# Windowed attention and a gated FFN on one core: two token tiles on one weight chunk, 24 float32 heads, decode moved beside the FFN

## The chip, the cores and the metric

One core of a Trainium2 chip. The metric is the device time of one launch in microseconds (us), the median of several runs. A profiled execution has a span, from its first to its last instruction, and its own device time, a little longer than that span.

## The reference, cut to what matters

Attention over 8 batches and 8 heads of size 64: 512 local tokens that see the 32 global tokens and a window of 32 on each side, and 32 global tokens that see everything. The 4608 x 512 result goes through an FFN whose weights have 512 x 2048 and 2048 x 512 numbers.

```python
s_ll = np.where(np.abs(pos[:, None] - pos[None, :]) <= 32, scale * q_l @ k_l.T, -1e9)
a_l = sm(np.concatenate([scale * q_l @ k_g.T, s_ll], axis=-1))
out_l = a_l @ np.concatenate([v_g, v_l], axis=2)
out_g = sm(scale * q_g @ k_all.T) @ v_all
x = np.concatenate([out_g, out_l], axis=2)        # then to 4608 x 512
h = x @ w_in
r = np.maximum(h, 0.0)
g = s * (r * r) + b
return g @ w_out
```

## The kernel before

**Units of work.** A slot j is one head on one half (256 rows) of a batch's local tokens: 128 slots, 16 to a batch. A tile t is 256 token rows of x, so eight slots fill one tile; tile 16 holds all the global tokens. The FFN runs in 136 steps m, eight to a tile: `ffn_in(m)` makes 256 hidden units of the tile (24 matmuls into PSUM tile `ps_h`), ACT takes the relu (`r`), DVE squares and scales it, ACT and DVE split it into a high and a low part (`g`), and `ffn_out(m)` adds it into two output accumulators (12 matmuls into `acc`). `ffn_out(m - 1)` stands behind `ffn_in(m)`, and slot j = m + 10 (`LAG`) is worked on beside step m.

**Two kinds of heads.** Slots from 16 (`NF`) on are split: each operand becomes a high and a low float32r part by an ACT copy and a DVE or POOL subtraction (`split`, `v_split`, `p_split`), and PE multiplies the parts. The first 16 slots, batch 0, go as float32, two heads at a time (`scores32`, `transposes32`, `pv32`): no splits, and ACT scales the probabilities.

**Weights.** They arrive as 64-bit words and are decoded on the chip (`weight_piece`): 32 pieces of 512 columns, each a 512 KB load, an ACT pass over the middle bits (L147), three DVE passes (L148, L151, L152), an ACT copy to the high part (L156) and a DVE subtraction for the low part (L157). All of `wi` and `wo` is used in the first eight steps, since those run through all hidden units of tile 0.

**Order.** Tile waits follow from the buffers. Up to slot 19 a scheduler orders every engine's queue at build time; from slot 20 (`ORDERED`), step 10, PE takes the order of the code. Every engine works its queue in order. [...] SP issues the loads, and each load waits for the eighth one before it to land. `keep_busy` runs matmuls on constants at the start.

## Time and profile before

| | |
|---|---|
| median of 3 runs | 1034.72 us (1034.71 to 1036.84) |
| the profiled execution's own time | 1035.21 us, 1.81 us more than its span |
| its span | 1033.4 us |
| PE busy | 998.6 us (97%) |
| DVE, ACT, POOL busy | 813.8 (79%), 710.4 (69%), 300.2 us (29%) |
| mean granted TensorE clock | 0.979 of full speed |

A line of the page's fifth part gives a group of equal instructions: line, engine, tile written <- tiles read, shape, count, then busy time, mean duration, and idle time before it with who ended that. A digit in a row of slices is the busy share in tenths. Durations of ACT and DVE overlap a little when they run back to back, so the distance from start to start is what one costs there.

### The profile page before, as it was taken

To read this page: it belongs to the slowest core of one execution; us is meant where nothing else is said; L and a number is where in the kernel's file an instruction comes from. 1 tells how busy PE (TensorE), PEld (TensorE's weight loads), DVE (VectorE), ACT (ScalarE), POOL (GpSimd) and SP (SyncE) were. 2 spreads that over 40 slices of the span, in tenths; PEclk is the share of its full clock that TensorE was granted. 3 is DMA by queue.
4 is the path that set the end of the run, shared out by engine and by line. 5 is a ranking of instruction groups with operands and counts; after the bars stand their busy time and mean duration, and the time that the engine had idled before them with its cause. 6 is when DMAs were issued, how large, how long until landed. Compare 5 with 4: busy or idle time off the path is not lost.

```text
span 1033.4 us, 20334 instructions
## 1 busy us (share of the span) xinstructions
PE 998.6 (97%) x7060; PEld 904.7 (88%) x7060; DVE 813.8 (79%) x2096; ACT 710.4 (69%) x1816; POOL 300.2 (29%) x365
## 2 busy tenths in 40 slices
PE   7779989999999999999999999999999999999996
...
GB/s 301 248 219 151 89 91 73 72 59 90 88 73 54 72 87 76 79 61 90 74 79 56 77 83 67 79 67 87 75 75 58 95 72 44 43 24 35 12 21 21
DMA packets 62254, 85.73 MB, mean 83 GB/s; under 512 B 7368, under 2 KB 49352, under 8 KB 62152
## 3 DMA queue, kind: packets, MB, share of 16 engines
...
q10 hardware_dynamic: 288, 1.05, 0.3%
...
## 4 chain that ended last, share of the span: by engine, by line
PE 85%; ACT 5%; DVE 5%; DMA 3%; issue 1%; SPq 0%; DVEq 0%; ACTq 0%
PE ps_h L499 34%; PE acc L532 34%; PE ps_t L308 5%; PE ps_o L380 4%; PE ps_s L355 4%; PE ps_og L451 2%; DMA wst<-in_w_out 2%; PE ps_g L359 1%; ACT sm L219 1%; ACT wst L147 1%; DVE g L514 1%; DVE x L393 1%; DMA b_t<-in_bv 1%; DVE r L506 1%; ACT g L513 1%
## 5 line engine op out<-in xcount | busy, mean ns | idle before, releaser
L499 PE MATMUL ps_h<-xs,wi 128*128 128x256 f32 x3264 | 419.3, 284 | 0.0
L532 PE MATMUL acc<-wo,g 128*128 128x512 f32 x1632 | 405.0, 395 | 0.5 <-ACT g L513 0.5
L499 PEld LDWEIGHTS ps_h<-xs,wi 128*128 128x128 f32 x3264 | 397.1, 190 | 3.3 <-issue 0.5
L532 PEld LDWEIGHTS acc<-wo,g 128*128 128x128 f32 x1632 | 294.9, 188 | 56.8 <-ACT g L513 0.8
L514 DVE SCALAR_TENSOR_TENSOR g<-r,b_t,g 128x512 fp32r<-128x512 f32 x136 | 120.3, 885 | 57.6 <-ACT g L513 57.0
L505 ACT ACTIVATE r<-ps_h 128x512 f32<-128x512 f32 x136 | 81.3, 598 | 115.5 <-PE ps_h L499 109.7
L513 ACT ACTIVATE g<-r,b_t 128x512 fp32r<-128x512 f32 x136 | 98.4, 723 | 78.6 <-DVE r L506 78.1
L192 POOL TENSOR_TENSOR kq<-rq,kq 128x256 fp32r<-128x256 f32 x112 | 83.9, 750 | 231.1 <-ACT kq L191 226.7
L506 DVE SCALAR_TENSOR_TENSOR r<-ps_h,s_t,r 128x512 f32<-128x512 f32 x136 | 101.2, 744 | 58.3 <-ACT r L505 58.3
L190 POOL TENSOR_TENSOR kq<-rk,kq 64x416 fp32r<-64x416 f32 x56 | 61.0, 1089 | 264.3 <-ACT kq L189 254.4
L219 ACT ACTIVATE sm<-sm,nm 128x224 f32<-128x224 f32 (+1 forms) x256 | 119.7, 469 | 1.4 <-DVE nm L213 1.0
L200 POOL TENSOR_TENSOR vs<-rv,vs 128x256 fp32r<-128x256 f32 x112 | 91.2, 815 | 51.2 <-ACT vs L199 45.9
L308 PE MATMUL ps_t<-ident,sm 128*128 128x128 f32 (+1 forms) x512 | 96.8, 277 | 7.9 <-DVE pg L433 3.0
L363 ACT COPY tg<-ps_g 32x256 f32<-32x256 f32 (+1 forms) x112 | 42.3, 378 | 72.3 <-PE ps_g L359 71.7
L380 PE MATMUL ps_o<-pt,vs 128*128 128x256 f32 x448 | 91.0, 285 | 0.0
L213 DVE CUSTOM_DVE_ANT_0 sm<-ps_s,mask 128x192 f32<-128x192 f32 (+1 forms) x224 | 74.6, 370 | 11.2 <-PE ps_s L355 11.0
L443 POOL TENSOR_TENSOR vsg<-rvg,vsg 128x320 fp32r<-128x320 f32 x64 | 57.8, 924 | 77.5 <-ACT vsg L442 77.5
L391 DVE TENSOR_TENSOR u<-ps_o,u 128x256 f32<-128x256 f32 x112 | 47.3, 422 | 41.8 <-ACT u L390 40.0
L355 PE MATMUL ps_s<-kq 128*128 128x192 f32 (+1 forms) x448 | 78.4, 266 | 0.0
L355 PEld LDWEIGHTS ps_s<-kq 128*128 128x128 f32 x448 | 72.0, 190 | 6.8
L308 PEld LDWEIGHTS ps_t<-ident,sm 128*128 128x128 f32 (+1 forms) x512 | 58.4, 145 | 13.3 <-ACT ptp L315 4.6
L228 DVE TENSOR_SCALAR sm<-sm,ss 128x192 f32<-128x192 f32 (+1 forms) x224 | 68.0, 346 | 1.0
...
## 6 DMA issues: line engine op xcount, KB each, us to landing
rq<-in_qd SPq DMA_DIRECT2D x112, 128.0 KB, 2.3
rv<-in_vw SPq DMA_DIRECT2D x112, 128.0 KB, 2.1
...
wst<-in_w_in SPq DMA_DIRECT2D x15, 512.0 KB, 4.3
wst<-in_w_out SPq DMA_DIRECT2D x15, 512.0 KB, 4.3
...
```

The source lines that it names most:

```text
L192: nc.gpsimd.tensor_sub(out=qs[:, 1, :], in0=rq, in1=f32(qs[:, 0, :]))
L200: nc.gpsimd.tensor_sub(out=vs[:, :, 1, :], in0=rv4, in1=f32(vs[:, :, 0, :]))
L219: nc.scalar.activation(out=p, in_=p, func=AF.Exp, bias=nm[:, n:n + 1], scale=-1.0, accum_out=ss[:, n:n + 1],)
L308: nc.tensor.transpose(out=p_t[:, at:at + q], in_=sm[0:q, c0:c0 + P], identity=ident[0:q, 0:q])
L355: nc.tensor.matmul(p_s[:, cols], lhsT=qs[:, a, blk * P:(blk + 1) * P], rhs=ks[:, cols], start=(a == 0), stop=(a == 1),)
L380: nc.tensor.matmul(p_o[:, blk, :, q0:q0 + n], lhsT=vs[:, 2 * blk + c], rhs=pt[:, :, o], start=(c == 1), stop=(c == 0),)
L499: nc.tensor.matmul(p_h[:, k], lhsT=wi[:, a, c, f * P:(f + 1) * P], rhs=xs[:, e, c, :], start=(n == 0), stop=(n == 11),)
L505: nc.scalar.activation(out=r, in_=p_h, func=AF.Relu)
L506: nc.vector.scalar_tensor_tensor(out=r, in0=p_h, scalar=s_t, in1=r, op0=ALU.mult, op1=ALU.mult)
L513: nc.scalar.activation(out=g[:, 0], in_=r, func=AF.Identity, bias=b_t)
L514: nc.vector.scalar_tensor_tensor(out=g[:, 1], in0=r, scalar=b_t, in1=f32(g[:, 0]), op0=ALU.add, op1=ALU.subtract,)
L532: nc.tensor.matmul(oacc[t][i], lhsT=g[:, a, k, i * P:(i + 1) * P], rhs=wo[:, e, f, :], start=(pr == 0 and n == 0), stop=(pr == 7 and n == 5),)
```

## The change

- **Two tiles to a chunk.** Steps 0 to 15 (`FIRST`) each take one chunk of 128 hidden units and run it for tiles 0 and 1: the same 24 and 12 matmuls as before, but into four output accumulators. These take the banks `acc0`, `acc1`, `h1` and `o`, so `ps_h` has one bank, `h0`, until step 16. Step m needs chunk m alone.
- **Chunks of 1024 columns.** 16 chunks in place of 32 pieces, 1 MB to a load, each with the same six passes at twice the width (L140 and L151 on ACT, L141, L144, L145, L152 on DVE). Four staging buffers; the load of chunk c + 4 waits for chunk c's last pass. Three chunks (`EARLY`) are called for among the first eight pairs and one at the end of each step from then on.
- **24 float32 slots.** Twelve pairs: eight ahead of step 0, the other four at steps 2, 5, 8 and 11 (scores), one step later (transposes) and one more (product with V). A pair's k, q and v come in one load of 606 KB (`load32`, `pairs`).
- **Order.** PE takes the code's order from step 0 on. Batch 0's global-token work is placed by `G_FIRST`, and V and the temporary of the decode (`wb`) share one buffer. The warming matmuls are 8 at the start and 16 behind the second pair's scores, and the activation table is asked for at the start (`act_first`).
- **Buffers.** `kq`, `rk` and `rq` go from three to two, `xs` from one to two; tiles get other paddings.

```diff
-NF = 16
-AHEAD = 0
+NF = 24
+FIRST = 16
 LAG = 10
-ORDERED = 20
-WARM_FIRST = 28
+WARM_FIRST = 8
+WARM_SECOND = 16
+SPARE = 12
+NCH = 16
+EARLY = (1, 4, 7)
+S32, T32, PV32 = ({3 * i + 2 + k: 8 + i for i in range(4)} for k in range(3))
+G_FIRST = {1: ("load", 0), 3: ("pv", 0), 4: ("pv", 2), 5: ("load", 4), 7: ("pv", 4), 9: ("pv", 6)}
...
+    def weight_load(c):
+        n = c if c >= SPARE else SPARE + c % 4
+        st = weight_tile(n, I32, f"wst{c}")[:, 0:2050]
+        nc.sync.dma_start(st.bitcast(I16)[:, 1:4097], wts[c])
+        st_["w", c] = st
...
+        below = sb.tile([P, 20 * D], I16, tag="rvg", name=f"wb{c}", bufs=1)[:, 0:1024]
...
     def ffn_in(m):
-        t, pr = m // 8, m % 8
-        xs = xs_[t]
-        p_h = ps.tile([P, 2, HALF], F32, tag="h", name=f"ps_h{m}", bufs=2)
+        if m < FIRST:
+            tag, terms = "h0", [(t, m) for t in range(2)]
+        else:
+            tag, terms = f"h{m % 2}", [(m // 8, 2 * (m % 8) + k) for k in range(2)]
+        p_h = ps.tile([P, 2, HALF], F32, tag=tag, name=f"ps_h{m}")
...
+            outs = [(0, i, [(i // 2, m)]) for i in range(4)]
+            tags = ("acc0", "acc1", "h1", "o")
...
+            for t, i, _ in sorted(outs, key=lambda x: -x[1] if m < FIRST else x[1]):
+                o = sb.tile([P, DM + 16], F32, tag="r", name=f"o{t}_{i}", bufs=2)[:, 0:DM]
+                (nc.vector.tensor_copy if i == 2 else nc.scalar.copy)(out=o, in_=oacc[t, i])
...
+    for i in range(10):
+        if i < 8:
+            scores32(i)
+        if 0 <= i - 1 < 8:
+            transposes32(i - 1)
+        if 0 <= i - 2:
+            pv32(i - 2)
+            if i - 2 == 3:
+                x_split(0)
+            elif i - 2 == 7:
+                x_split(1)
+        if i >= 8:
+            g_softmax(0, i - 8)
+        if i in EARLY:
+            next_chunk()
+    fixed.enter_context(tc.manual_schedule(engines={mybir.EngineType.PE}))
...
+        if m < NM:
+            ffn_in(m)
...
         if 0 <= m - 1 < NM:
-            ffn_out(m - 1, turns.pop(j, iter(())))
+            ffn_out(m - 1, turn)
+        list(turn)
+        if m < FIRST:
+            next_chunk()
```

ACT's queue around the first relu of the FFN. `wst` is a staged piece or chunk, `ptp` a pair's transposed probabilities, `xs` the split x, `r0` and `g0` step 0. Before, pieces 0 to 22 stand ahead of `r0`:

```order
L329 COPY x1_669<-ps_op4_660 128x256 [waits DVE_49,PE_49]
L147 ACTIVATE wst22_624<-wst22_624,mid_b_129 128x512 [waits DMAHW2_49]
L156 CAST wo_127<-we19_576 128x512 [waits DVE_49]
L505 ACTIVATE r0_698<-ps_h0_673 128x512 [waits PE_49]
L156 CAST wi_126<-we20_607 128x4x128 [waits DVE_49]
L156 CAST wo_127<-we17_519 128x512 [waits DVE_49]
L315 COPY ptp5_731<-ps_t10_732 128x416 [waits PE_49]
L147 ACTIVATE wst21_615<-wst21_615,mid_b_129 128x512 [waits DMAHW4_49,Activation_49]
L505 ACTIVATE r1_769<-ps_h1_744 128x512 [waits PE_49]
L513 ACTIVATE g0_701<-r0_698,b_t_72 128x512 [waits DVE_49]
```

Now, with chunk 8 of 16 before and chunk 9 behind `r0`, and the last pairs' copies between:

```order
L309 COPY ptp6_536<-ps_t13_543 128x416 [waits PE_49]
L140 ACTIVATE wst8_742<-wst8_742,mid_b_112 128x1024 [waits DMAHW7_49]
L309 COPY ptp7_569<-ps_t14_570 128x416 [waits PE_49]
L151 CAST w5_820<-wst5_401 128x1024 [waits PE_49]
L309 COPY ptp7_569<-ps_t15_576 128x416 [waits PE_49]
L469 CAST xs1_610<-x1_507 128x512 [waits DVE_49]
L506 ACTIVATE r0_650<-ps_h0_625 128x512 [waits PE_49]
L509 ACTIVATE g0_653<-r0_650,b_t_72 128x512 [waits DVE_49]
L140 ACTIVATE wst9_823<-wst9_823,mid_b_112 128x1024 [waits DMAHW1_49,Activation_49]
L506 ACTIVATE r1_693<-ps_h1_668 128x512 [waits PE_49]
```

The first pass over chunks 6, 7 and 8 and the whole of chunks 0 to 5 stand ahead of `r0`; the pass over chunk 9 moved between `g0` and `r1`.

DVE's queue between `r4` and `r5`; `wb`, `we` and `wst` belong to the decode. Before:

```order
L506 SCALAR_TENSOR_TENSOR r4_1057<-ps_h4_1032,s_t_71,r4_1057 128x512 [waits Activation_49]
L157 TENSOR_TENSOR wo_127<-we27_799,wo_127 128x512 [waits Activation_49]
L157 TENSOR_TENSOR wo_127<-we25_723,wo_127 128x512 [waits Activation_49]
L151 SCALAR_TENSOR_TENSOR wst30_915<-wst30_915,we30_916 128x512 [waits DVE_49]
L157 TENSOR_TENSOR wi_126<-we28_808,wi_126 128x4x128 [waits Activation_49]
L190 TENSOR_TENSOR kq16_1075<-rk16_989,kq16_1075 64x416 [waits Activation_49]
L148 TENSOR_SCALAR we31_925<-wst31_924 128x512 [waits DMAHW2_49,DVE_49]
L148 TENSOR_SCALAR we29_907<-wst29_906 128x512 [waits DMAHW1_49,DVE_49]
L152 SCALAR_TENSOR_TENSOR we30_916<-wst30_915 128x512 [waits DVE_49]
L151 SCALAR_TENSOR_TENSOR wst31_924<-wst31_924,we31_925 128x512 [waits DVE_49]
L514 SCALAR_TENSOR_TENSOR g4_1060<-r4_1057,b_t_72,g4_1060 128x512 [waits Activation_49]
L151 SCALAR_TENSOR_TENSOR wst29_906<-wst29_906,we29_907 128x512 [waits DVE_49]
L506 SCALAR_TENSOR_TENSOR r5_1123<-ps_h5_1098,s_t_71,r5_1123 128x512 [waits Activation_49]
```

Now, the last seven rows ahead of `r5` and the four behind it:

```order
L141 TENSOR_SCALAR wb8_1075<-wst8_742 128x1024 [waits DMAHW7_49,DMAHW4_49,Pool_49]
L152 TENSOR_TENSOR w7_993<-wst7_666,w7_993 128x1024 [waits Activation_49]
L144 SCALAR_TENSOR_TENSOR wst8_742<-wst8_742,wb8_1075 128x1024 [waits DVE_49]
L217 TENSOR_SCALAR ss18_1007<-ss18_1007 128x4 [waits Activation_49]
L145 SCALAR_TENSOR_TENSOR wst8_742<-wst8_742 128x1024 [waits DVE_49]
L141 TENSOR_SCALAR wb9_1153<-wst9_823 128x1024 [waits DMAHW1_49]
L218 RECIPROCAL ss18_1007<-ss18_1007 128x4 [waits DVE_49]
L507 SCALAR_TENSOR_TENSOR r5_1050<-ps_h5_1025,s_t_71,r5_1050 128x512 [waits Activation_49]
L144 SCALAR_TENSOR_TENSOR wst9_823<-wst9_823,wb9_1153 128x1024 [waits DVE_49]
L152 TENSOR_TENSOR w8_1080<-wst8_742,w8_1080 128x1024 [waits Activation_49]
L145 SCALAR_TENSOR_TENSOR wst9_823<-wst9_823 128x1024 [waits DVE_49]
L510 SCALAR_TENSOR_TENSOR g5_1053<-r5_1050,b_t_72,g5_1053 128x512 [waits Activation_49]
```

The passes over chunks 6 to 15 and the work of four pairs now stand between the `r` and `g` rows of steps 1 to 13; before, pieces 20 to 31 stood between those of steps 0 to 6.

PE's queue at steps 4 to 6. Before, `ps_h4` and `ps_h5` lie in two banks and follow each other:

```order
L499 MATMUL ps_h4_1032<-xs0_597,wi_126 128x256 [waits DVE_49]
L499 MATMUL ps_h4_1032<-xs0_597,wi_126 128x256 x23
L499 MATMUL ps_h5_1098<-xs0_597,wi_126 128x256 [waits DVE_49]
L499 MATMUL ps_h5_1098<-xs0_597,wi_126 128x256 x5
L323 MATMUL ps_op6_1022<-ptp6_933,rvp6_671 64x128 [waits Activation_49]
L323 MATMUL ps_op6_1022<-ptp6_933,rvp6_671 64x96 x2
L323 MATMUL ps_op6_1022<-ptp6_933,rvp6_671 64x128 x2
L323 MATMUL ps_op6_1022<-ptp6_933,rvp6_671 64x64 x2
L532 MATMUL acc0_0_775<-wo_127,g3_974 128x512 [waits Activation_49]
L532 MATMUL acc0_0_775<-wo_127,g3_974 128x512
L532 MATMUL acc0_1_776<-wo_127,g3_974 128x512 x2
L499 MATMUL ps_h5_1098<-xs0_597,wi_126 128x256 x17
```

Now step 5's and step 6's input halves lie in one bank, and `ps_h6` waits for DVE's `r5`:

```order
L499 MATMUL ps_h5_1025<-xs0_453,w5_820 128x256 x12
L499 MATMUL ps_h5_1025<-xs1_610,w5_820 128x256 x12
L537 MATMUL acc0_0_706<-w4_739,g4_943 128x512 [waits Activation_49]
L537 MATMUL acc0_0_706<-w4_739,g4_943 128x512
L537 MATMUL acc0_0_706<-w4_739,g4_943 128x512 [waits DVE_49]
L537 MATMUL acc0_1_707<-w4_739,g4_943 128x512 x3
L537 MATMUL acc0_2_708<-w4_739,g4_943 128x512 x3
L537 MATMUL acc0_3_709<-w4_739,g4_943 128x512 x3
L499 MATMUL ps_h6_1085<-xs0_453,w6_910 128x256 [waits DVE_49]
L499 MATMUL ps_h6_1085<-xs0_453,w6_910 128x256 x11
L499 MATMUL ps_h6_1085<-xs1_610,w6_910 128x256 x12
```

The input half of a step moved behind the output half of the step two before it, and its first matmul waits for the read of the step before.

## Rows read from the trace of the kernel before

**Rows 1.** The page's slices of the whole span: PE's busy tenths, 40 slices of 25.8 us.

```profile
PE   7779989999999999999999999999999999999996
```

**Rows 2.** Busy time of each engine in stretches of the start: stretch, its length, then PE, PEld, DVE, ACT and POOL busy us (instructions), granted clock, DMA share, GB/s.

```profile
10.00:20.00 10.00, 5.38 (x30) 2.89 (x30) 7.79 (x29) 7.75 (x22) 0.00 (x0) 0.82 1.00 365
...
130.00:140.00 10.00, 6.88 (x41) 5.80 (x40) 7.95 (x17) 7.54 (x19) 5.54 (x7) 0.79 0.41 125
140.00:150.00 10.00, 10.00 (x72) 9.51 (x71) 7.54 (x17) 6.10 (x18) 4.44 (x6) 0.86 0.28 82
```

**Rows 3.** The same view in two longer stretches, same columns.

```profile
20.00:50.00 30.00, 22.50 (x117) 13.99 (x116) 29.51 (x82) 29.79 (x79) 0.00 (x0) 0.67 0.81 267
50.00:70.00 20.00, 15.36 (x108) 12.16 (x107) 19.52 (x49) 18.56 (x43) 0.00 (x0) 0.82 0.69 216
```

**Rows 4.** PE's matmuls in order of time, 133 to 142 us: start us, us, line, out<-in, tile, count, and in brackets the idle time before and who ended it.

```profile
133.46 0.33 PE L359 MATMUL ps_g<-kq,qgs 128*64 128x256 f32 x1
136.24 0.48 PE L428 MATMUL ps_tg<-ident,sg 128*128 128x128 f32 x1 [2.44 <-DVE sg L364]
```

**Rows 5.** PE's matmuls in order of time, 139 to 187 us, same columns; an FFN input half is x24, an output half x12.

```profile
139.68 4.43 PE L499 MATMUL ps_h<-xs,wi 128*128 128x256 f32 x24
...
148.62 3.04 PE L499 MATMUL ps_h<-xs,wi 128*128 128x256 f32 x24
...
182.63 0.47 PE L355 MATMUL ps_s<-kq 128*128 128x224 f32 x3
...
183.17 0.40 PE L380 MATMUL ps_o<-pt,vs 128*128 128x256 f32 x2
...
183.91 3.05 PE L499 MATMUL ps_h<-xs,wi 128*128 128x256 f32 x24
186.79 2.94 PE L532 MATMUL acc<-wo,g 128*128 128x512 f32 x12
```

**Rows 6.** All engines in order of time, the first 14 us: start us, us, engine, line, out<-in, idle before.

```profile
5.69 0.43 DVE L148 TENSOR_SCALAR we<-wst 128x512 int16<-128x512 int16 x1 [4.29 <-DMA wst<-in_w_in]
...
8.89 0.69 DVE L151 SCALAR_TENSOR_TENSOR wst<-wst,we 128x512 int32<-128x512 int16 x1
...
9.51 0.68 DVE L157 TENSOR_TENSOR wi<-we,wi 128x512 fp32r<-128x512 f32 x1
...
10.11 0.68 DVE L152 SCALAR_TENSOR_TENSOR we<-wst 128x512 int32<-128x512 int32 x1
...
10.69 0.43 PE L277 MATMUL ps_sp<-rkp,rqp 64*128 64x192 f32 x1
...
11.32 0.35 PE L277 MATMUL ps_hp<-rkp,rqp 64*128 64x224 f32 x1
...
12.89 0.43 DVE L148 TENSOR_SCALAR we<-wst 128x512 int16<-128x512 int16 x1 [0.73 <-DMA wst<-in_w_in]
13.24 0.35 DVE L213 CUSTOM_DVE_ANT_0 sm<-ps_sp,mask 128x192 f32<-128x192 f32 x1
...
13.63 0.46 ACT L219 ACTIVATE sm<-sm,nm 128x192 f32<-128x192 f32 x1
```

**Rows 7.** ACT in order of time, 36 to 42 us, where it never waits: start us, us, line, out<-in.

```profile
36.08 1.53 ACT L226 ACTIVATE sm<-sm,ss 128x192 f32<-128x192 f32 x4
37.51 0.75 ACT L147 ACTIVATE wst<-wst,mid_b 128x512 int32<-128x512 uint32 x1
38.16 0.60 ACT L156 CAST wi<-we 128x512 fp32r<-128x512 f32 x1
38.67 0.49 ACT L315 COPY ptp<-ps_t 128x416 f32<-128x416 f32 x1
39.07 0.75 ACT L416 ACTIVATE sg<-sg,gm 128x544 f32<-128x544 f32 x1
...
40.93 0.37 ACT L286 COPY sg<-ps_gp 64x288 f32<-64x288 f32 x1
41.21 0.48 ACT L219 ACTIVATE sm<-sm,nm 128x224 f32<-128x224 f32 x1
...
41.69 0.60 ACT L156 CAST wo<-we 128x512 fp32r<-128x512 f32 x1
```

**Rows 8.** The page's DMA issues: line, engine, count, KB each, median us from issue to landing.

```profile
wst<-in_w_in SPq DMA_DIRECT2D x15, 512.0 KB, 4.3
```

**Rows 9.** The chain of work that ended last, in order of time: start us, us, engine, tile, line, count.

```profile
72.86 0.93 PE ps_op L323 x11
...
87.01 0.39 PE ps_t L308 x4
...
117.94 0.60 PE ps_og L451 x10
...
155.82 2.80 PE ps_h L499 x24
...
159.22 2.79 PE acc L532 x12
```

**Rows 10.** The page's costliest groups, two of DVE: line, out<-in, count, busy us, mean ns of one, idle before.

```profile
L514 DVE SCALAR_TENSOR_TENSOR g<-r,b_t,g 128x512 fp32r<-128x512 f32 x136 | 120.3, 885 | 57.6 <-ACT g L513 57.0
...
L506 DVE SCALAR_TENSOR_TENSOR r<-ps_h,s_t,r 128x512 f32<-128x512 f32 x136 | 101.2, 744 | 58.3 <-ACT r L505 58.3
```

**Rows 11.** DVE's groups by shape, 20 to 60 us: line, out<-in, count, busy us, mean ns of one.

```profile
L331 DVE COPY x<-ps_op 128x256 f32<-128x256 f32 x4 | 1.7, 416 | 0.0
```

More of the change, by code (lines that the diff above doesn't have):

```diff
@@ L282, in scores32 @@
         nc.tensor.matmul(
-            p_g[0:64, 0:ng], lhsT=st_["rqg", 0][:, 64 * hp:64 * hp + 64], rhs=own(rk, hf), start=True, stop=True,
+            p_g[0:64, 0:ng], lhsT=st_["rqgp", b][:, 64 * hp:64 * hp + 64], rhs=own(rk, hf), start=True, stop=True,
         )
+        if i == 1:
+            with tc.issue_after(part.ins):
+                keep_busy(WARM_SECOND, "warm1")
         softmax(heads, p_s)
@@ L562, in window_attention_then_ffn @@
                 extra[s0 + G_TR + G_PV[i]].append(lambda b=b, h=h: g_pv(b, h))
-    def pick(pair, split_one):
-        def run(j):
-            if NF <= j < NS:
-                split_one(j)
-            elif 0 <= j < NF and j % 2 == 0:
-                with tc.high_priority(offset=AHEAD):
-                    pair(j // 2)
-        return run
-    ld = pick(load32, load)
-    sp = pick(lambda i: None, split)
-    vl, vl32 = pick(lambda i: None, v_load), pick(v_load32, lambda j: None)
-    sc = pick(scores32, scores)
@@ L577, in window_attention_then_ffn, with pick @@
-    tr = pick(transposes32, lambda j: None)
-    vsp = pick(lambda i: None, v_split)
-    pvs = pick(pv32, lambda j: None)
-    piece = 0
-    qg_load(0)
-    ld(0)
-    ld(2)
-    fixed = ExitStack()
-    for j in range(NM + LAG + 2):
-        if j == ORDERED:
-            fixed.enter_context(tc.manual_schedule(engines={mybir.EngineType.PE}))
+    def pick(run):
+        return lambda j: run(j) if NF <= j < NS else None
+    ld, sp, vl, sc, vsp = (pick(run) for run in (load, split, v_load, scores, v_split))
```

302 lines of the change are left out of this document (161 added, 141 removed).

## The prediction

> **What bounds the kernel now.** I read the slices of the span first [rows 1]: PE's busy share is 9 tenths or more in nearly every slice behind the first six, so there PE is the limit, and a change of the start can only move the moment from which PE runs without a gap. Then the start by stretches [rows 2, 3]: from 20 to 50 us ACT is busy for 29.79 of 30 us and DVE for 29.51, PE for 22.5 at a granted clock of 0.67. ACT and DVE, which decode the weights and do the softmax, set the time there. The last disturbance is near 136 us: PE stands still for 2.44 us behind DVE [rows 4], the mean clock of that stretch is 0.79 and of the next 0.86 [rows 2], and step 10's input half takes 4.43 us where step 11's takes 3.04 [rows 5].
>
> From then on the two programs do the same work on PE, so I compare them at one point: the start of step 15's output half, 186.79 us in the trace of before [rows 5] (the change puts step 16's input half ahead of a product and four transposes there, and I count those in). What the change gains there it keeps to the end.
>
> **Term 1: the first FFN step can start.** Step 0 now needs tiles 0 and 1, so all eight pairs. In the trace of before the first scores run at 10.69 us and end at 11.67, yet DVE reads them at 13.24, behind a decoding pass that waited for its load until 12.89, and ACT's first exponential is at 13.63 [rows 6]. Now the first pair's 606 KB is the first load. The 512 KB piece that was the first load of before was ready at 5.69 [rows 6]; I take 6.0 for the pair, 0.97 for scores and 0.35 for the first DVE pass, and put the first exponential at 7.3.
>
> From there ACT is the longest list ahead of `r0`. The order gives the counts, the distances from start to start the prices [rows 7]: 32 exponentials at 0.48 with their sums (15.4 us), 32 scalings at 0.36 (11.4), 8 score copies at 0.28 (2.2), 16 copies of transposes at 0.40 (6.4), two long exponentials (1.5), four casts of x at 0.51 (2.0), four small V casts (1.3). A decoding pass costs 0.65 and a cast 0.51 for 512 columns. A 288-column copy lasts 0.37 and a 512-column cast 0.60, which is 1.0 ns for each further column, so 1024 columns should cost 1.15 and 1.0; the bounds are one price of 512 and twice that price. Nine passes and six casts: 10.4 and 6.0. Sum 56.6 us. ACT idled 1.65 us in the 50 us from 20 to 70 [rows 3]: 2 more. Behind the last scaling come transposes, two copies, the product, a DVE copy, the last cast and six matmuls, about 3 us beyond what is counted. The input half of step 0 ends at 7.3 + 56.6 + 2 + 3 = **69 us**.
>
> That is hardly earlier than before, where PE's unbroken work begins at 72.86 [rows 8]: "decoded beside the FFN" holds for ten chunks, while six stand whole ahead of `r0` and three more with their first pass. Two things can make it later. A chunk's load is 1 MB: half of it lands in 4.3 us [rows 9], and at the 365 GB/s of 10 to 20 us [rows 2] the other half adds 1.4, so 5.7, bounds 4.3 and 8.6. The pass over chunk 8 stands on ACT ahead of the last pair's copies; its load waits for chunk 4's last pass, some 7 us ahead of it by the list, so it just about hides, and any more is paid. And SP's queue holds nine pairs and four chunks, 9.7 MB, ahead of the small loads and chunk 4: 27 us at that rate, near 36 us with what stands between, when ACT comes to chunk 4. I take 69, from 64 (if part of the nine passes fills gaps that ACT would have had) to 73.
>
> **Term 2: PE's own work from there to the point.** At full clock [rows 8]: 16 input halves at 2.80 (44.8), 15 output halves at 2.79 (41.9). Four pairs: scores 0.97 [rows 6], one more product at 0.35, two times four transposes at 0.39, the product with V at 0.93 [rows 8], 3.03 each, 12.1. Four global products at 0.60 (2.4), ten global transposes at the same 0.39 for four (1.0). Slots 24 to 26: scores at 0.54 and one set of product and transposes at 0.74 [rows 5], with the first four transposes 2.7. Sum **104.9 us**. The eight slots that are no longer split would have cost PE 0.54 and 0.74 each [rows 5], 10.2 in all against the 12.1, so PE's work hardly changes; what falls away is DVE's, ACT's and POOL's splitting.
>
> **Term 3: PE waits for DVE in steps 4 to 13.** Until step 16 `ps_h` has one bank, so a step's input half waits until DVE has read the step before (`r`), and only an output half and a pair's work stand between. DVE prices: at 512 columns 0.62 and 0.60 from start to start, the first pass 0.35 [rows 6]; a 256-column copy lasts 0.42 [rows 11] and a 512-column pass 0.68, again 1.0 ns a column, so the wide passes cost 1.14 and the first 0.62 (bounds 0.6 and 1.24, 0.35 and 0.70). `r` lasts 0.74, `g` 0.89 [rows 10]. From `r4` to `r11` the order has 8 first passes, 25 wide ones, seven `r`, seven `g`, 12 score passes at 0.35 and some 16 small ones: 5.0 + 28.5 + 5.2 + 6.2 + 4.2 + 5 = 54 us. PE's own work from the end of input half 4 to that of 11 is seven steps at 5.59, 8.3 of pairs and 2.3 of global work: 49.7. So 4.3 us of wait at the least. Taken step by step it is more: between `r4` and `r5` DVE has 12.6 us of this against PE's 8.6, and between `r9` and `r11` 20 against 13.6, while in steps 0 to 3 DVE stands idle, because chunk 6 needs the buffer that a load of V fills. With what each piles up I come to 9. I take **6.5**, the middle, bounds 2 and 13.
>
> In the trace of before a queue holds back what is ready behind what is not: the scores of 11.67 waited for a load that they don't need [rows 6]. [...]
>
> **Term 4: the clock.** A stall near 2.4 us was followed by a half at 4.43 in place of 3.04 [rows 4, 5], 1.4 lost. At 69 us PE comes from a stretch like the one before, where the mean was 0.67 to 0.82 [rows 3]. I take **2**, bounds 0 and 6.
>
> [...]
>
> **Term 5: four accumulators are emptied at once.** Two `r` buffers carry four output tiles, so the third waits for the first one's store, and output half 16 for the fourth copy. Between lies a slot's PE work and an input half, 4.1 us. I take **1**, bounds 0 and 3. I put `kq`, `rk` and `rq` with two buffers at nothing: a load that lands in less than the 4.3 us of 512 KB [rows 9] has a step of 6.9 us to do it in, and if that cover were gone each late load would show as a wait of a score.
>
> **The sum.** 69 + 104.9 + 6.5 + 2 + 1 = 183.4, against 186.8: 3.4 us earlier. The profiled execution of 1035.21 would become 1031.8, the median of 1034.72 becomes **1031.3 us**.
>
> **The rivals.** *DVE decides and PE's clock falls* (slower). One bank, and chunk passes ahead of nearly each `r` of steps 4 to 13: 12 us of wait and three falls of the clock, 4.2. Sum 69 + 104.9 + 12 + 4.2 + 1 = 191.1, 1039.0 us. It decides from 11.9 us of waits and clock together on (186.8 less the other terms). For it: DVE's 54 us against 49.7, and the stall at 136 us, also behind DVE. Against it: each step has an output half of 2.79 us [rows 8] between a read and the matmul that waits for it, and over the eight steps DVE's work is only 4.3 us more than PE's.
>
> *The start is short* (faster by much). The passes ahead of `r0` fill gaps of ACT, which waited where I have it busy: 64 for term 1, 4 for term 3, 1 for each other. 174.9, 1022.8 us. For it: the wide passes could cost less than my line from 256 to 512 columns. Against it: ACT's gaps in the trace are 1.65 us in 50.
>
> *The change does not do what it says* (no gain). Chunk 4 or 8 lands late, ACT stands before it with all pairs' work behind, and the start moves to 72.5: 186.9, 1034.8 us. For it: ACT and DVE before waited for such loads until 12.89 [rows 6]. Against it: it needs only 5.7 us of load hidden.
>
> **How the numbers follow.** Forecast 0.36, slower rival 0.28, short start 0.20, no gain 0.16. Measurements of this kernel tell a change of some 0.2% (2.1 us) from none. Of the forecast I count 0.26 as faster, 0.08 as the same and 0.02 as slower, of the last rival 0.12 as the same and 0.04 as slower: faster 0.46, same 0.20, slower 0.34. The likeliest case by itself spans 1027 to 1035. The range for 8 in 10 takes in the short start and the slower rival with half of its bounds: 1022 to 1042.
>
> **What would show it.** The input half of step 0 ends at 64 to 73 us (term 1), ACT above 95% busy from 12 to 65 us. PE's idle time behind `r` (`ps_h` waiting for DVE) in steps 4 to 13 adds up to 2 to 13 us, most of it ahead of steps 6, 11 and 12 (term 3). The clock is below 1 at the start of the FFN and at most twice after it (term 4). Output half 15 starts near 183 us, and the steps behind it last 6.9 us as before; if they are longer, the two-buffer tiles cost what I put at nothing. An input half 0 that ends before 60 us, or waits over 15 us, would prove the sum wrong.

## The result, and the profile after

| | before | after |
|---|---|---|
| median | 1035.78 us (4 runs beside after's) | 1043.38 us (1043.0 to 1044.45, 4 runs) |
| ratio, 95% interval | | 1.0074 (1.0059 to 1.0088) |
| span of the profiled execution | 1033.4 us | 1042.4 us |
| PE, DVE, ACT busy | 998.6, 813.8, 710.4 us | 1007.8, 774.3, 697.7 us |

The change makes the kernel 7.6 us slower; the forecast was 1031.3 us, the range 1022 to 1042. DVE has 39.5 us less to do and ACT 12.7, PE 9.2 more.

Busy time by stretches in the kernel after: stretch, its length, PE, PEld, DVE, ACT, POOL, granted clock, DMA share, GB/s.

```profile
7.30:71.30 64.00, 53.34 (x302) 34.51 (x302) 44.10 (x120) 56.27 (x145) 3.79 (x4) 0.75 0.65 255
20.00:50.00 30.00, 25.48 (x135) 15.84 (x134) 21.15 (x66) 29.31 (x78) 3.79 (x4) 0.67 0.75 291
50.00:70.00 20.00, 15.96 (x106) 12.10 (x106) 12.66 (x27) 14.73 (x35) 0.00 (x0) 0.76 0.26 86
60.00:90.00 30.00, 25.59 (x155) 21.17 (x155) 10.82 (x26) 15.59 (x33) 0.00 (x0) 0.83 0.18 70
...
140.00:160.00 20.00, 17.87 (x123) 14.39 (x121) 19.94 (x31) 13.09 (x26) 2.92 (x2) 1.00 0.34 121
```

Against [rows 3], DVE is no longer full at the start, ACT still is until 50 us. DVE is idle for 19 of 30 us between 60 and 90 us and full from 140 to 160: the decode has moved beside the FFN, but not evenly. The profiled execution of after is the slowest of its four (1044.45 us).

PE's queue in the kernel after, in order of time: start us, us, line, out<-in, count, idle time before and who ended it.

```profile
69.85 1.44 PE L499 MATMUL ps_h<-xs,w 128*128 128x256 f32 x5 [0.34 <-DVE xs L470]
72.76 4.78 PE L499 MATMUL ps_h<-xs,w 128*128 128x256 f32 x24 [1.47 <-DVE r L507]
...
88.31 2.97 PE L499 MATMUL ps_h<-xs,w 128*128 128x256 f32 x24
92.86 0.78 PE L448 MATMUL ps_og<-vsg,pg 128*64 128x128 f32 x10 [0.75 <-ACT ptp L309]
...
103.81 0.43 PE L268 MATMUL ps_sp<-rp 64*128 64x192 f32 x1 [0.17 <-DVE og L453]
105.29 3.07 PE L499 MATMUL ps_h<-xs,w 128*128 128x256 f32 x24
113.40 4.63 PE L499 MATMUL ps_h<-xs,w 128*128 128x256 f32 x24 [2.30 <-DVE r L507]
...
142.07 0.78 PE L448 MATMUL ps_og<-vsg,pg 128*64 128x128 f32 x10 [1.80 <-ACT ptp L309]
...
161.19 3.07 PE L499 MATMUL ps_h<-xs,w 128*128 128x256 f32 x24 [1.52 <-DVE r L507]
164.10 0.99 PE L302 MATMUL ps_t<-ident,sm 128*128 128x128 f32 x8
164.85 2.99 PE L537 MATMUL acc<-w,g 128*128 128x512 f32 x12
167.68 2.96 PE L499 MATMUL ps_h<-xs,w 128*128 128x256 f32 x24
...
191.02 2.98 PE L537 MATMUL acc<-w,g 128*128 128x512 f32 x12
...
199.87 3.04 PE L537 MATMUL acc<-w,g 128*128 128x512 f32 x12 [1.26 <-ACT o L545]
204.02 3.05 PE L499 MATMUL ps_h<-xs,w 128*128 128x256 f32 x24
```

Input half 0 ends at 71.3 us (69.85 + 1.44). Output half 15, the point of comparison, starts at 191.02 against 186.79 [rows 5], 4.2 us late. Step 18's input half starts at 204.02 against 197.77 in the trace of before, 6.25 late, and the last one at 1024.77 against 1015.91, 8.86 late. So the start and the first sixteen steps lose 4.2, the emptying of the accumulators 2.0, and 2.6 more are lost later, where PE's list shows no new wait.

DVE and ACT ahead of `r5`, for which the input half at 113.40 waits, in the kernel after (L506 is ACT's relu, L507 DVE's part of `r`):

```profile
107.79 0.69 DVE L141 TENSOR_SCALAR wb<-wst 128x1024 int16<-128x1024 int16 x1 [0.86 <-POOL vsg L440]
108.40 1.22 DVE L152 TENSOR_TENSOR w<-wst,w 128x1024 fp32r<-128x1024 f32 x1
...
109.50 1.26 ACT L140 ACTIVATE wst<-wst,mid_b 128x1024 int32<-128x1024 uint32 x1
109.53 1.22 DVE L144 SCALAR_TENSOR_TENSOR wst<-wst,wb 128x1024 int32<-128x1024 int16 x1
...
110.67 0.57 ACT L506 ACTIVATE r<-ps_h 128x512 f32<-128x512 f32 x1
110.79 1.23 DVE L145 SCALAR_TENSOR_TENSOR wst<-wst 128x1024 int32<-128x1024 int32 x1
111.93 0.69 DVE L141 TENSOR_SCALAR wb<-wst 128x1024 int16<-128x1024 int16 x1
...
112.62 0.72 DVE L507 SCALAR_TENSOR_TENSOR r<-ps_h,s_t,r 128x512 f32<-128x512 f32 x1
```

Input half 5 was complete near 108.2 (105.29 + 2.91), and `r5` ran at 112.62, behind five passes of chunks 7, 8 and 9. The first of them had waited for POOL to leave the buffer that `wb` shares with a load of V. DVE is not alone: ACT's relu ended at 111.24, behind a pair's exponentials and the pass over chunk 9, so with DVE free `r5` would still have run there, 1.4 us earlier and no more.

**The 2.6 us of the later batches.** Lining up the input halves of both traces, the distance grows by 0.2 us at two steps of each batch and nowhere else. One is step 21, in the kernel after (all engines):

```profile
224.74 3.06 PE L499 MATMUL ps_h<-xs,w 128*128 128x256 f32 x24
...
225.71 1.08 POOL L184 TENSOR_TENSOR kq<-rk,kq 64x416 fp32r<-64x416 f32 x1
...
226.87 0.74 POOL L186 TENSOR_TENSOR kq<-rq,kq 128x256 fp32r<-128x256 f32 x1
227.17 0.72 DVE L390 TENSOR_TENSOR x<-u 64x256 f32<-64x256 f32 x1
...
227.56 0.93 POOL L195 TENSOR_TENSOR vs<-rv,vs 128x256 fp32r<-128x256 f32 x1
...
228.00 0.52 DVE L217 TENSOR_SCALAR ss<-ss 128x2 f32<-128x2 f32 x1
...
228.64 0.57 DVE L367 TENSOR_TENSOR pt<-ps_t,pt 128x416 fp32r<-128x416 f32 x1
229.26 0.42 PEld L425 LDWEIGHTS ps_tg<-ident,sg 128*128 128x128 f32 x4 [0.41 <-DVE pt L367]
```

and the same step before:

```profile
218.50 3.06 PE L499 MATMUL ps_h<-xs,wi 128*128 128x256 f32 x24
...
220.06 0.58 DVE L190 TENSOR_TENSOR kq<-rk,kq 64x416 fp32r<-64x416 f32 x1
...
220.57 0.74 POOL L200 TENSOR_TENSOR vs<-rv,vs 128x256 fp32r<-128x256 f32 x1 [0.44 <-ACT vs L199]
...
221.37 0.42 DVE L393 TENSOR_TENSOR x<-u 64x256 f32<-64x256 f32 x1
...
221.91 0.57 DVE L370 TENSOR_TENSOR pt<-ps_t,pt 128x416 fp32r<-128x416 f32 x1
222.66 0.59 PEld L428 LDWEIGHTS ps_tg<-ident,sg 128*128 128x128 f32 x4
```

Four global transposes need the bank `ps_t`, which DVE reads last (`pt`). Counted from the step's input half that read starts 0.49 us later than before (3.90 against 3.41), since K's split of an odd slot, POOL's (64x416), now falls into this step, where before DVE split an even one. It moves POOL's other work to where DVE adds u to x: that pass takes 0.72 in place of 0.42, and the next, over 128x2 values, 0.52. The wait stands in the weight load's row, not in the matmul's, so PE's list of waits hides it.

### The profile page after: what moved, and what is told of

Its sections match the earlier page's. It is cut to its first block, busy times and chain, and to the rows that moved or that the text cites. A ratio compares the mean times of both kernels' runs of the same rounds, so it can differ in the third digit from the quotient of the medians.

```text
span 1042.4 us, 20149 instructions
## 1 busy us (share of the span) xinstructions
PE 1007.8 (97%) x7088; PEld 904.8 (87%) x7088; DVE 774.3 (74%) x1981; ACT 697.7 (67%) x1760; POOL 292.2 (28%) x345
## 4 chain that ended last, share of the span: by engine, by line
PE 75%; DVE 13%; ACT 7%; issue 3%; DMA 1%; POOL 0%; SPq 0%; DVEq 0%; ACTq 0%
PE ps_h L499 31%; PE acc L537 30%; PE ps_t L302 4%; PE ps_s L352 3%; PE ps_o L377 3%; DVE g L510 2%; PE ps_og L448 1%; DVE r L507 1%; DVE wst L144 1%; ACT sm L214 1%; PE ps_g L356 1%; DVE sm L223 1%; DVE x L390 1%; ACT g L509 1%; ACT sm L221 1%
## 5 line engine op out<-in xcount | busy, mean ns | idle before, releaser
L499 PE MATMUL ps_h<-xs,w 128*128 128x256 f32 x3264 | 420.0, 285 | 8.1 <-DVE r L507 5.3
L499 PEld LDWEIGHTS ps_h<-xs,w 128*128 128x128 f32 x3264 | 398.4, 191 | 14.1 <-DVE r L507 6.6
L537 PE MATMUL acc<-w,g 128*128 128x512 f32 x1632 | 404.8, 395 | 1.3 <-ACT o L545 1.3
L537 PEld LDWEIGHTS acc<-w,g 128*128 128x128 f32 x1632 | 295.4, 188 | 58.3 <-ACT o L545 1.5
L507 DVE SCALAR_TENSOR_TENSOR r<-ps_h,s_t,r 128x512 f32<-128x512 f32 x136 | 101.3, 745 | 81.2 <-ACT r L506 80.8
L506 ACT ACTIVATE r<-ps_h 128x512 f32<-128x512 f32 x136 | 81.2, 597 | 111.7 <-PE ps_h L499 103.0
L195 POOL TENSOR_TENSOR vs<-rv,vs 128x256 fp32r<-128x256 f32 x104 | 92.9, 893 | 70.7 <-ACT vs L194 69.8
L184 POOL TENSOR_TENSOR kq<-rk,kq 64x416 fp32r<-64x416 f32 x52 | 56.3, 1082 | 141.0 <-ACT kq L183 129.1
L377 PE MATMUL ps_o<-pt,vs 128*128 128x256 f32 (+2 forms) x416 | 84.1, 284 | 0.2 <-ACT o L545 0.2
L208 DVE CUSTOM_DVE_ANT_0 sm<-ps_s,mask 128x224 f32<-128x224 f32 (+1 forms) x208 | 69.0, 369 | 9.0 <-PE ps_s L352 8.8
L352 PE MATMUL ps_s<-kq 128*128 128x224 f32 (+1 forms) x416 | 72.5, 265 | 0.0
L352 PEld LDWEIGHTS ps_s<-kq 128*128 128x128 f32 x416 | 66.8, 189 | 6.5
L360 ACT COPY tg<-ps_g 32x288 f32<-32x288 f32 (+1 forms) x104 | 39.3, 378 | 46.3 <-PE ps_g L356 45.0
L377 PEld LDWEIGHTS ps_o<-pt,vs 128*128 128x128 f32 x416 | 63.0, 191 | 0.6 <-ACT o L545 0.4
```

The costliest lines, as they stand in the source:

```text
L195: nc.gpsimd.tensor_sub(out=vs[:, :, 1, :], in0=rv4, in1=f32(vs[:, :, 0, :]))
L352: nc.tensor.matmul(p_s[:, cols], lhsT=qs[:, a, blk * P:(blk + 1) * P], rhs=ks[:, cols], start=(a == 0), stop=(a == 1),)
L377: nc.tensor.matmul(p_o[:, blk, :, q0:q0 + n], lhsT=vs[:, 2 * blk + c], rhs=pt[:, :, o], start=(c == 1), stop=(c == 0),)
L499: nc.tensor.matmul(p_h[:, k], lhsT=wi[f][:, a, c, :], rhs=xs_[t][:, e, c, :], start=(n == 0), stop=(n == 11),)
L506: nc.scalar.activation(out=r, in_=p_h, func=AF.Relu)
L507: nc.vector.scalar_tensor_tensor(out=r, in0=p_h, scalar=s_t, in1=r, op0=ALU.mult, op1=ALU.mult)
```

## The experiments

All times are medians; each ratio is against the kernel before on the same chip.

| run | edit | us | ratio, 95% interval |
|---|---|---|---|
| e1_flip | after, K's low part on POOL for even slots | 1040.81 | 1.0047 (1.0034 to 1.0060) |
| e2_before_two | before, `kq`, `rk`, `rq` with two buffers | 1051.58 | 1.0145 (1.0129 to 1.0162) |
| e8_before_two_same_place | the same, wider, other tiles 32 bytes lower | 1052.30 | 1.0170 (1.0153 to 1.0187) |
| e11_before_two_exact | the same, other tiles at before's addresses | 1040.12 | 1.0044 (1.0029 to 1.0058) |
| e12_before_shift32 | before, tiles 32 bytes higher | 1039.17 | 1.0044 (1.0026 to 1.0061) |
| e3_light_dve | after, less decode on DVE | 1039.58 | 1.0043 (1.0028 to 1.0058) |
| e4_light_act | after, less decode on ACT | 1041.71 | 1.0050 (1.0037 to 1.0064) |
| e5_own_wb | after, own buffer for `wb` | 1048.37 | 1.0134 (1.0117 to 1.0151) |
| e6_warm | after, eight warming matmuls | 1044.45 | 1.0091 (1.0071 to 1.0112) |
| e7_own_flip_warm | e5, e1 and e6 together | 1044.94 | 1.0102 (1.0086 to 1.0119) |
| e9_even | e5, DVE and ACT in the code's order | 1066.93 | 1.0303 (1.0284 to 1.0321) |
| e10_even_flip | e9 and e1 | 1061.62 | 1.0255 (1.0235 to 1.0274) |
| e13_behind_g5 | e5, chunk c behind step c - 5's `g` | 1038.15 | 1.0021 (1.0010 to 1.0032) |
| e14_behind_g4 | e5, chunk c behind step c - 4's `g` | 1032.31 | 0.9970 (0.9957 to 0.9982) |
| e15_three_edits | e13, e1 and e18 | 1035.62 | 1.0002 (0.9991 to 1.0013) |
| e16_g4_and_two | e14, e1 and e18 | 1030.00 | 0.9953 (0.9935 to 0.9971) |
| e17_g3_and_two | chunk c behind step c - 3's `g`, e1 and e18 | 1028.59 | 0.9938 (0.9918 to 0.9958) |
| e18_flush | after, two more buffers for output copies | 1043.31 | 1.0079 (1.0059 to 1.0098) |

**Two buffers.** e1_flip:

```diff
-K_POOL = lambda j: j % 2
+K_POOL = lambda j: 1 - j % 2
```

> The changed kernel with one number flipped: POOL takes the low part of K for even slots and DVE for odd ones, where it was the other way round. Theory (POOL beside DVE): from step 20 on the changed kernel loses 0.2 us at each of two steps in a batch, since with two kq buffers the split of an odd slot, POOL's, now falls beside the global transposes; there DVE's passes last longer and the four transposes wait for its read of ps_t. With the flip DVE does that split itself and the 0.2 us are gone: 2.6 us faster than the changed kernel, about 1040.8 us, and the steps from 30 on run as in the kernel before. Rival (padding and addresses, or fewer loads in flight): the flip does nothing there, 1043.4 us, or costs what DVE then does more, up to 0.3 us at each step with K.

2.6 us faster, as the theory had it, but only in part for its reason: the 0.2 us are gone at one of the two steps of a batch (1.2 us in all), not at both. Ahead of step 18 the wait of output half 16 fell from 1.26 to 0.51 us and that of step 12 from 1.52 to 1.12. In its trace input half 1 also begins 1.65 us earlier; e18, which has no flip, has 1.36 of that, so most of it is not the flip's. e2, e8 and e11 ask for the cause in the kernel before:

```diff
-        rk = sb.tile([P, 480], F32, tag="rk", name=f"rk{j}", bufs=3)[:, 0:NC]
+        rk = sb.tile([P, 480], F32, tag="rk", name=f"rk{j}", bufs=2)[:, 0:NC]
...
-        kq = sb.tile([P, 1026], F32R, tag="kq", name=f"kq{j}", bufs=3)
+        kq = sb.tile([P, 1026], F32R, tag="kq", name=f"kq{j}", bufs=2)
```

> The kernel before with two buffers for kq, rk and rq in place of three, and nothing else. Theory (POOL beside DVE): the same loss of 0.2 us at two steps in each batch appears, 2.6 to 3 us slower than before, about 1038.5 us. Rival (the loss comes from something else in the change): no difference behind step 20, and at most a little in the start, where pieces of weights use the same buffers; 1035 to 1036 us.

Neither: 16 us slower, 0.1 us in every step, with no new wait of PE. Every later tile had moved, so the next runs held the places.

> The kernel before with two buffers for kq, rk and rq, each half as wide again as it was, so that every other tile keeps its place. In the run with two buffers of the old width PE lost 0.1 us in every step, with matmuls of ps_h at 285 ns in place of 283 and of acc at 399 in place of 394, though PE waited for nothing. Theory (where tiles lie sets what a matmul takes; the buffer count costs the two places in a batch): matmuls are at 283 and 394 again, and the loss is 0.2 us at two steps in each batch from step 20 on, some 1.5 to 3 us in all: 1037 to 1038.5 us. Rival (two buffers slow each step by themselves): 0.1 us in each step again, 1048 us or more.

> The kernel before with two buffers for kq, rk and rq, half as wide again, and xr 32 bytes wider, so that xs, g, pt, vs, r and the weights lie at the very addresses of before; in the earlier run of this kind they lay 32 bytes lower. Theory (the addresses of the FFN's operands set the 0.1 us in each step, the buffer count does not): matmuls of ps_h at 283 and of acc at 394 ns again, and a loss only at two steps of each batch, 1.5 to 3 us: 1036.5 to 1038.5 us. Rival (two buffers cost each step 0.1 us): 1048 to 1053 us.

> The kernel before with xr 32 bytes wider and nothing else: three buffers as before, every tile behind xr 32 bytes higher. Theory (addresses): matmuls of acc at 397 ns or more in place of 394, 0.05 to 0.15 us in every step, 1042 to 1052 us. Rival (the buffer count): no difference, 1035 us.

PE's groups by shape from 300 to 950 us (count, busy us, mean ns of one, idle): in the kernel before, e8, e11 and e12, the output half's matmul.

```profile
L532 PE MATMUL acc<-wo,g 128*128 128x512 f32 x1092 | 270.3, 394 | 0.0
```

```profile
L532 PE MATMUL acc<-wo,g 128*128 128x512 f32 x1071 | 269.1, 398 | 0.0
```

```profile
L532 PE MATMUL acc<-wo,g 128*128 128x512 f32 x1085 | 268.9, 395 | 0.0
```

```profile
L532 PE MATMUL acc<-wo,g 128*128 128x512 f32 x1091 | 273.7, 398 | 0.0
```

e8 fell to the rival by its time, but its tiles lay 32 bytes lower. With the places kept (e11) the matmul is back, and what is left is 0.2 us at two steps of each batch, 2.44 us from step 21 to the end, and 1.4 ahead of it (1.6 more in all than the range had). That is the late loss of the change, made in the kernel before by the buffer count alone: at step 21 POOL does the 64x416 split there too, and `pt` is read 3.89 us behind the start of the input half. At the other step, 25, the flip leaves the loss (3.95 in e1, 3.72 before); what it consists of there is not shown. e12 shows the other half: with three buffers and tiles 32 bytes higher a step takes 7.07 us in place of 7.03, 4.7 us from step 21 to the end, and the median is 3.4 higher, less than the theory's range.

**Decode.** e3_light_dve cuts two DVE passes to 64 columns for chunks 6 to 15; e4_light_act leaves out ACT's pass over chunks 3 to 8:

```diff
+        n = 1024 if c < 6 else 64
...
-        nc.scalar.activation(out=mid, in_=mid.bitcast(U32), func=AF.Relu, bias=mid_b, scale=2.0**-13)
+        if not 3 <= c <= 8:
+            nc.scalar.activation(out=mid, in_=mid.bitcast(U32), func=AF.Relu, bias=mid_b, scale=2.0**-13)
```

> The changed kernel with two of DVE's four decoding passes cut to 64 columns for chunks 6 to 15, so that the weights of these chunks are not the reference's; some 18 us of DVE less beside steps 0 to 13. Theory (DVE's queue makes PE wait and the waits cost the clock): the waits behind r at steps 6 and 12 and behind the copies at step 10, 5.6 us together, fall to under 2, and the low clock of input half 6 goes with them: 5 to 7 us faster than the changed kernel, 1037 to 1038.5 us. Rival (one ps_h bank, the round PE, ACT, DVE, PE itself is too long): the waits stay within 2 us of what they are and the time is 1041.5 to 1043.5 us.

3.8 us faster, between the two: the waits of steps 6, 10 and 12 went from 5.62 to 3.21 us (1.39, 1.62, 0.20), and input half 6 took 3.08 in place of 4.63. What is left of step 6's wait is ACT's: in this trace its relu of half 5 starts at 109.02, behind a pair's exponentials, and DVE's `r5` follows at 109.63.

> The changed kernel without ACT's decoding pass over chunks 3 to 8, so that the weights of these chunks are not the reference's; 7.4 us of ACT less ahead of step 0. Theory of the prediction (ACT's list ahead of r0 sets the start): input half 0 ends 5 to 7 us earlier than at 71.3 us and the kernel is as much faster, 1036.5 to 1038.5 us. Rival (the chain of the last pairs sets it, since ACT idles some 5 us between 50 and 70 us): only the pass over chunk 8, which stands ahead of a copy that PE waits for, is gained, 1 to 2 us, 1041.5 to 1042.5 us.

The time is the rival's, the start the theory's. In e4 (ACT and PE in order of time):

```profile
64.86 1.44 PE L501 MATMUL ps_h<-xs,w 128*128 128x256 f32 x5 [0.34 <-DVE xs L472]
66.83 1.19 ACT L141 ACTIVATE wst<-wst,mid_b 128x1024 int32<-128x1024 uint32 x1 [2.74 <-DMA wst<-in_wts]
67.92 0.58 ACT L508 ACTIVATE r<-ps_h 128x512 f32<-128x512 f32 x1
...
69.34 2.08 PE L501 MATMUL ps_h<-xs,w 128*128 128x256 f32 x8 [3.04 <-DVE r L509]
```

Input half 0 ends at 66.3, 5.0 earlier than in the changed kernel's trace and 3.3 to 5.3 earlier than in the traces that have the same start (69.6 to 71.6 in e1, e3, e6 and e18): ACT's list sets most of the start. But now a pass that waits 2.74 us for its load stands ahead of `r0`, and step 2 starts only 2.7 us earlier. ACT's queue paid for what stood in it, so the next runs move the passes.

**Place.** e5_own_wb:

```diff
-        below = sb.tile([P, 20 * D], I16, tag="rvg", name=f"wb{c}", bufs=1)[:, 0:1024]
+        below = sb.tile([P, 1024 if c < 15 else 20 * D], I16, tag="qgs" if c < 15 else "rvg", name=f"wb{c}", bufs=1)[:, 0:1024]
```

> The changed kernel with the decode's temporary wb of chunks 0 to 14 in the buffer of qgs, which is idle until step 12, in place of the buffer that a load of V fills too. DVE, which is busy for 4 of 10 us or less between 60 and 90 us, can then run the passes over chunks 6 to 11 ahead of r4. Theory (the decode arrives late because it waits for a buffer, and then stands ahead of r): the waits of steps 4 to 12 (0.75, 2.30, 1.80, 1.52 us) and the low clock of input half 6 shrink by 4 to 6 us, some of it paid back ahead of r0 to r2 (up to 2 us): 1038.5 to 1041 us. Rival (the work only moves: each pass ahead of an early r costs what it cost ahead of a late one): 1042.5 to 1045 us.

5 us slower, outside both ranges. The passes of chunks 6 to 8 now stand ahead of `xs1`, input half 0 ends at 77.7, and the 6.8 us that its trace wins back between steps 3 and 12 don't make up for it. e6_warm:

> The changed kernel with eight more warming matmuls on constants between the input halves of steps 0 and 1, where PE waits 1.47 us. Theory (the wait behind a half-busy stretch costs the clock): input half 1 runs at 2.9 to 3.5 us in place of 4.78, the eight matmuls cover the wait and 0.3 to 1.5 us more; 0.5 to 1.5 us faster than the changed kernel, 1042 to 1043 us. Rival (the clock follows the whole stretch from 55 us on, not this wait): input half 1 stays above 4.3 us and the time is 1043.5 to 1045 us.

Input half 1 took 3.72 in place of 4.78 us, but began 1.7 later: no gain. The wait is not what lowered the clock: the granted clock is 0.50 already from 69.8 to 71.3 us in the changed kernel, ahead of the wait, and from 62.0 to 71.5 in e6, ahead of the eight matmuls. e7_own_flip_warm had e5's loss in it and came to neither number, 1044.94 us:

> The changed kernel with three edits together: wb in its own buffer, K's low part on POOL for even slots, eight warming matmuls behind input half 0. If the three losses are separate, their gains add: 2.6 for the flip, as its run showed, 3 to 4 for the buffer, about 1 for the clock: 1035 to 1037 us, as fast as the kernel before. If the buffer only moves work, 1040 to 1041 us.

e9_even has only chunks 0 to 2 ahead, and DVE and ACT in the order of the code up to step 14:

```diff
+    beside.enter_context(tc.manual_schedule(engines={mybir.EngineType.DVE, mybir.EngineType.Activation}))
```

> The changed kernel with the decode spread evenly: only chunks 0 to 2 stand ahead of step 0, and DVE and ACT take the order of the code from step 0 to step 14, where each step has the first four passes over one chunk, and the last two over the chunk before, behind its own r and g; wb as in the run with its own buffer. Theory (the sum of the decode is small enough, its place is what costs): input half 0 ends near 65 us in place of 71.3, since three hi casts and six first passes of ACT fall from its list, each step of 1 to 13 waits for DVE by about the same 0 to 1 us, and the clock stays up: 5 to 10 us faster than the changed kernel, 1033 to 1038 us. Rival (DVE's work beside steps 0 to 13 is the bound, wherever it stands): what the start gains the steps lose, 1041 to 1046 us.

31 us slower than the kernel before. Step 2 begins 6.5 us earlier than in the changed kernel, and then it loses 30 us to steps 2 to 16, though in no stretch DVE, ACT or PE is full. From input half 1 to 16 PE's list has 27.7 us of waits in place of 8.0, and five input halves take 4.31 to 5.49 us. ACT at step 2:

```profile
82.00 1.54 ACT L225 ACTIVATE sm<-sm,ss 128x192 f32<-128x192 f32 x4 [0.51 <-DVE ss L222]
...
83.70 0.59 ACT L510 ACTIVATE r<-ps_h 128x512 f32<-128x512 f32 x1
...
85.13 1.10 PE L503 MATMUL ps_h<-xs,w 128*128 128x256 f32 x7 [3.21 <-DVE r L511]
```

A pair's whole softmax, with its own waits for DVE, stands ahead of `r2`. That is neither of the two expectations: not the sum of DVE's work, but another thing ahead of `r`. With the flip (e10_even_flip) it is 5.3 us less, where 2 to 2.6 were expected; why is open. So the order was given back to the scheduler, `wb` kept its own buffer, and only this was fixed: a chunk's first pass on ACT and DVE may not stand ahead of the `g` of an earlier step.

```diff
+        after = behind[c - 4] if c >= 4 else None
+        with tc.issue_after(after[0].ins) if after else nullcontext():
+            nc.scalar.activation(out=mid, in_=mid.bitcast(U32), func=AF.Relu, bias=mid_b, scale=2.0**-13)
+        with tc.issue_after(after[1].ins) if after else nullcontext():
+            nc.vector.tensor_scalar(
```

> The changed kernel with wb in its own buffer, and the first passes over chunk c (from chunk 5 on) queued behind step c - 5's g on ACT and on DVE; everything else is left to the scheduler. The order has one chunk beside each step from 0 to 10, where the changed kernel has none beside steps 0 to 3 and two between r4 and r5. Theory (the place of the passes costs, not their sum): input half 0 ends 3 to 5 us earlier than at 71.3 us, the waits behind r of steps 4 to 12 fall from 5.6 to under 3 us: 5 to 8 us faster than the changed kernel, 1035.5 to 1038.5 us. Rival (the sum of the decode beside the FFN is the bound): the waits return in other steps, 1041 to 1045 us.

> The same with chunks from 4 on queued behind step c - 4's g: one chunk fewer ahead of step 0 and each a step later. Theory (place): the start gains 1 to 2 us more than with the run behind step c - 5's g, and as long as no input half waits for its weights the time is 1 us lower, 1034.5 to 1038 us. Rival (each pass that leaves the start is paid again beside a step): within 1 us of that run or slower.

5.2 and 11.1 us faster than the changed kernel. e13 lies in its range, e14 2.2 us below its own, and it beats the kernel before. e13's trace has three waits for DVE, of 1.07 us (`pg`, ahead of input half 2), 1.17 (`r`, 3) and 1.62 (`r`, 12); in e14's the first is 0.26 and the others are gone, which no run explains. Its stretches and PE's queue:

```profile
60.00:90.00 30.00, 25.77 (x170) 21.89 (x171) 22.20 (x37) 19.03 (x37) 0.28 (x1) 0.94 0.27 91
...
140.00:160.00 20.00, 20.00 (x142) 17.39 (x141) 16.09 (x27) 15.35 (x32) 4.45 (x5) 1.00 0.13 35
```

```profile
64.58 0.86 PE L502 MATMUL ps_h<-xs,w 128*128 128x256 f32 x5 [0.34 <-DVE xs L473]
66.91 4.43 PE L502 MATMUL ps_h<-xs,w 128*128 128x256 f32 x24 [1.48 <-DVE r L510]
...
105.20 2.97 PE L502 MATMUL ps_h<-xs,w 128*128 128x256 f32 x24
```

DVE is busy for 22.2 us between 60 and 90, where it was for 10.8, and 16.1 between 140 and 160, where it was full. Input half 0 ends at 65.4, 5.9 earlier than in the changed kernel's trace; behind step 1 no input half waits for `r`. The decoding work is the same as in the changed kernel; what differs is the place of `wb` (alone in e5, slower) and the order of the queues. No run has that order without `wb`'s own buffer.

> The run behind step c - 5's g, with K's low part on POOL for even slots, and with two more buffers (those of vsg and pg) for the four output tiles that are emptied behind step 15. If the losses are separate they add: 2.6 us for the flip and 1 to 1.5 for the wait of output half 16 behind the copies (1.26 us) come off that run's time: 1031.5 to 1035 us, faster than the kernel before by up to 4 us. If the early steps' loss stays, 1037 to 1041 us.

> The run behind step c - 4's g (1032.3 us) with K's low part on POOL for even slots and two more buffers for the output copies. If the losses are separate, 2.5 us less, as between the two runs behind step c - 5's g: 1029 to 1031 us, 4 to 6 us faster than the kernel before. If not, 1032 us.

> The same, with chunks from 3 on queued behind step c - 3's g, so that chunk 3 leaves the start too and every chunk has one step less in hand. Theory (each chunk that leaves the list ahead of r0 brings the start forward): 1 to 2 us less than with step c - 4's, 1027.5 to 1030 us. Rival (the passes now come too late, and input halves wait for their weights): 1031 us or more.

> The changed kernel with the last two of the four output tiles behind step 15 in the buffers of vsg and pg, in place of a second turn of the two r buffers, and nothing else. Output half 16 waits 1.26 us and a product 0.20 us behind these copies. Theory (the copies wait for the first ones' stores): 1.0 to 1.5 us faster, 1042 to 1042.4 us. Rival (the four copies stand on ACT and DVE ahead of r16 anyway): no difference.

e18's trace has no wait of output half 16 any more (1.5 us there), but its median can't be told from the changed kernel's. e15 is 2.5 us faster than e13, where 3.6 to 4.1 were expected; the two edits overlap, since the flip by itself shortens the same wait (e1). e16 is 2.3 faster than e14, in its range. e17 is the fastest, 6.4 us faster than the kernel before; from e16 its interval doesn't part it.

## Why the prediction was wrong

| step of the prediction | forecast | measured | 
|---|---|---|
| term 1, input half 0 ends | 69 (64 to 73) | 71.3 |
| term 2, PE's own work | 104.9 | 108.4 |
| term 3, waits for DVE in steps 4 to 13; measured: all waits of PE in steps 0 to 13 | 6.5 (2 to 13) | 8.0 |
| term 4, the clock | 2 (0 to 6) | 3.4 |
| term 5 and what follows up to step 18 | 1 (0 to 3) | 2.0 |
| two buffers for `kq`, `rk`, `rq` | 0 | 2.6 |

The waits are those in PE's list above up to 161.19 (1.47, 0.75, 0.17, 2.30, 1.80, 1.52). The clock's price is 4.78 - 2.97 and 4.63 - 3.08. Term 2 is what is left of 191.02 - 71.3. The measured terms are 12.3 us above the forecast ones: 3.4 us earlier became 8.9 later in the two profiled executions (7.6 by the medians).

- **The step that failed outright** is "I put `kq`, `rk` and `rq` with two buffers at nothing". I asked only whether a load lands in time. What the third buffer gave was the place of POOL's split in time; without it POOL runs beside DVE where PE waits for DVE's read (e11, at one of the two steps). Of the two signs that I had named, the wait of a score did not come, the loss stands in the weight loads of transposes; the other, longer steps behind output half 15, did.
- **Term 2 was mis-sized by 3.5 us.** I took a half's busy time from the chain, 2.80 and 2.79 (that is [rows 9], and the 512 KB load [rows 8]; the prediction has the two numbers exchanged). The distance from start to start, as from 161.19 to 164.10 (2.91) and from 164.85 to 167.68 (2.83), is 2.88 and 2.87 on average at the full clock: 1.2 and 1.3 us more. The four pairs take the rest, 13.3 us in place of 12.1, most of it in their scores with the global product.
- **Terms 1, 3, 4 and 5** lay within their bounds, all on the late side. In term 1 ACT's work was right: it is busy for 56.3 us from 7.3 to 71.3 (forecast 56.6) and idle for 7.7 (forecast 5). About 1.4 of the 2.3 us too many belong to this execution: from 60 to 68 us its granted clock is 0.79, in e18, with the same start, 1.00, and there input half 0 ends at 69.9. The mechanism of term 1 (ACT's list) is shown by e4, e13 and e14, which have fewer passes in it and start earlier, that of term 3 (passes ahead of `r`, because chunk 6's buffer comes free late) by e3, e13 and e14. Of the 8.0 us only 3.8 are waits for `r` at steps 6 and 12; 2.55 are waits for ACT's copies of a pair, which I had not listed, and 1.47 is the round of the single bank at step 1. Even at step 6 a part is ACT's (e3).
- **The rival "DVE decides and PE's clock falls"** named the right engine and the wrong reason. Waits and clock came to 11.4 us, just under the 11.9 from which it was to decide. It took the sum of DVE's work as given; e14 has the same sum and no such wait. DVE had the time, 19 us of it between 60 and 90, and the queue's order did not use it.
- **The order of the queues**, which term 3 took from the scores of 11.67 [rows 6], said more than the sum of the work: `r5` ran at 112.62, behind five passes on DVE, and the 11.1 us between the changed kernel and e14, which has the same passes in another order and `wb` in its own buffer, fit it. Of the rival's three falls of the clock one came. Of the four longest waits only the 2.30 us has one behind it: the granted clock goes from 1.00 (112 to 114 us) to 0.52 (114 to 116). Behind the 1.80 and the 1.52 it stays at 1.00, and at the 1.47 it was low already (0.50).

Not settled: why e13 has three waits that e14 has not, what the buffer count costs at step 25, and what the two tiles to a chunk and the four late pairs would cost each by itself, since no run has one without the other.
